# Replicating 1/std of one batch over the partitions: by two steps of small DMAs instead of six matmuls

## The chip, the cores and the metric

One core of a Trainium2 chip. The metric is device time of one execution in microseconds (us), lower is better. Differences are judged on runs of the fast state; a ratio is the mean time of one kernel's fast runs over that of the other's of the same rounds, so it is not quite the ratio of the medians that are quoted beside it.

Names used below: PE is TensorE, ACT ScalarE, DVE VectorE, POOL GpSimd, SP SyncE. "Landing" of a DMA is counted from its issue to the moment its last data is in place. "L476" is a line of the kernel that the line is from; the changed kernel is shorter, so the same statement has another number there.

## The reference, cut to what matters

```python
B, N, D = 2, 256, 1152
mod = (_silu(c) @ w_mod).reshape(B, 6, 1, D)
shift_a, scale_a, gate_a, ... = [mod[:, i] for i in range(6)]
h = _layernorm(x, axis=-1) * (1 + scale_a) + shift_a
qkv = h @ wqkv
q, k, v = ...
p = _softmax(jnp.einsum('bqd,bkd->bqk', q, k) * D ** (-0.5), axis=-1)
a = jnp.einsum('bqk,bkd->bqd', p, v) @ wo
return x + gate_a * a
```

All weights and x are bf16. h is kept transposed: features on the partitions, tokens along the free dimension. 1/std is one number per token. It comes out of ScalarE as a column, one token per partition, and is needed as a row that stands on all 128 partitions.

## The kernel before: the parts concerned

For batch 0 the kernel centres x, transposes it, and starts the key matmuls before 1/std is known (the keys of that batch are scaled later, in the scores). 1/std enters h by a multiply on DVE. The row for this multiply, `rep_sb`, is made by PE: POOL splits 1/std into three bf16 parts, and six matmuls with the identity replicate them and add them up in PSUM bank 7.

```python
def rep(b):                       # six matmuls
    for i in (2 * b, 2 * b + 1):
        for n in range(3):
            lhs = bass.AP(rpart_sb, n * TT + i, [[3 * TT, P], [0, P]])
            lo = NTOK + (i % 2) * P
            op(PE, lambda pe, ...: pe.matmul(ps[7][:, lo:lo + P], lhs, ident[:, :],
                                             start=(n == 0), stop=(n == 2)), ...)

def rep_out(b):                   # copy to SBUF
    op(AC, lambda a: a.activation(rep_sb[:, b * NTOK:(b + 1) * NTOK], ps[7][:, NTOK:2 * NTOK], ACT.Copy), ...)

def norm_x(cc, b):                # the multiply that needs it
    op(DVE, lambda e: e.tensor_tensor(dst, src, rep_sb[:, b * NTOK:(b + 1) * NTOK], ALU.mult), ...)
# ... [cut]
for g in range(2, len(SGROUPS)):  # key matmuls of columns 0..6, features k = 4..8
    for k in range(a, b_):
        for j in range(NA):
            qk_mm("ka", h0T_sb, "h0", DC + j, k, j)
            ...
        b = k - 6
        if b in CENTRED:          # after k = 6
            rep(b)
            rep_out(b)
            for cc in range(0, 6):
                norm_x(cc, b)
        if k == DC - 2:
            h_mm(0)               # shift of features 0, 1, into bank 7
h_ev(0)                           # DVE: copy of the shift, frees bank 7
# ... [cut]
for j in range(NA):
    qk_evac(j, DC + j, j)         # DVE and ACT in turn
shift_group(0)
for cc in range(6, 9):
    norm_x(cc, 0)
for n, bank in enumerate((7, 0)): # "kb": the last two key columns
    for k in range(DC):
        qk_mm("kb", h0T_sb, "h0", DC + NA + n, k, bank)
    qk_evac(n, DC + NA + n, bank)
# then the query matmuls, which read hT_sb
```

Each engine runs its own list in order, and a helper adds the semaphore waits. DVE's order: six multiplies, then the shift copy, then the key evacuations.

## Time and profile before

| | |
|---|---|
| time before, three runs | 98.52 us median (98.29 to 99.14) |
| execution that was profiled | 242.59 us, span 240.8 us, slow |
| PE busy in that profile | 237.4 us (99%) |
| six replicating matmuls in its chain | 1.00 us |

In a chain of waits a line is: start, length, what, xcount. In a timeline it is: start, length, engine, line, operation, output<-input, shapes, xcount, and in brackets how long the engine sat idle before and who ended that. The lines that matter are shown in the prediction. The odd thing is that the profiled execution took almost 2.5 times as long as the timed ones, with PE slow throughout. Its granted clock is printed as 1.0.

### The profile page before, as it was taken

To read this page: it belongs to the slowest core of one execution; us is meant where nothing else is said; L and a number is where in the kernel's file an instruction comes from. 1 tells how busy PE (TensorE), PEld (TensorE's weight loads), DVE (VectorE), ACT (ScalarE), POOL (GpSimd) and SP (SyncE) were. 2 spreads that over 40 slices of the span, in tenths; PEclk is the share of its full clock that TensorE was granted. 3 is DMA by queue.
4 is the path that set the end of the run, shared out by engine and by line. 5 is a ranking of instruction groups with operands and counts; after the bars stand their busy time and mean duration, and the time that the engine had idled before them with its cause. 6 is when DMAs were issued, how large, how long until landed. Compare 5 with 4: busy or idle time off the path is not lost.

```text
span 240.8 us, 1836 instructions
## 1 busy us (share of the span) xinstructions
PE 237.4 (99%) x738; PEld 99.8 (41%) x738; DVE 50.3 (21%) x136; ACT 29.7 (12%) x64; POOL 12.1 (5%) x35
## 2 busy tenths in 40 slices
PE   8999999999999999999999999999999999999996
PEld 1885543332233323222344644533345433333443
DVE  3550031055105000041000530000002212351212
ACT  4559000001000000020000220000003100000000
POOL 2221032000003000000000000000000000000000
DMA  6999999930005600000000010066400001010101
GB/s 214 334 330 323 377 362 380 390 139 0 0 0 179 262 3 0 0 0 0 1 0 0 14 33 0 0 29 39 33 0 0 0 16 33 16 33 16 35 16 33
DMA packets 20092, 21.91 MB, mean 91 GB/s; under 512 B 2034, under 2 KB 16114, under 8 KB 20084
## 3 DMA queue, kind: packets, MB, share of 16 engines
q1 hardware_dynamic: 19936, 21.50, 30.8%
q10 hardware_dynamic: 148, 0.30, 0.4%
q8 instruction: 6, 0.10, 0.2%
q14 instruction: 2, 0.02, 0.0%
HBM read 19.76 MB, written 1.18 MB: 87 GB/s over the span
## 4 chain that ended last, share of the span: by engine, by line
PE 99%; DVE 0%; issue 0%
PE psbank L561 40%; PE psbank L855 20%; PE psbank L739 20%; PE psbank L817 4%; PE psbank L752 4%; PE psbank L334 2%; PE psbank L395 2%; PE psbank L493 1%; PE psbank L796 1%; PE psbank L411 1%; PE psbank L516 1%; PE psbank L476 0%; PE psbank L576 0%; DVE xo_sb L860 0%; DVE warm_sb L322 0%
## 5 line engine op out<-in xcount | busy, mean ns | idle before, releaser
L561 PE MATMUL psbank<-pvT_sb,wq_sb 128*128 128x512 bf16 (+2 forms) x111 | 48.8, 666 | 0.0
L739 PE MATMUL psbank<-wq_sb,hT_sb 128*128 128x384 bf16 x108 | 48.8, 685 | 0.0
L561 PE MATMUL psbank<-hT_sb,wq_sb 128*128 128x512 bf16 x81 | 48.6, 833 | 0.0
L855 PE MATMUL psbank<-wm_sb,pvT_sb 128*128 128x384 bf16 x99 | 44.4, 687 | 0.0
L739 PEld LDWEIGHTS psbank<-wq_sb,hT_sb 128*128 128x128 bf16 x108 | 18.7, 174 | 29.4 <-issue 29.1
L561 PEld LDWEIGHTS psbank<-pvT_sb,wq_sb 128*128 128x128 bf16 x111 | 17.7, 171 | 25.8 <-issue 21.8
L855 PEld LDWEIGHTS psbank<-wm_sb,pvT_sb 128*128 128x128 bf16 x99 | 17.3, 175 | 26.7 <-issue 26.4
L561 PEld LDWEIGHTS psbank<-hT_sb,wq_sb 128*128 128x128 bf16 x81 | 13.8, 172 | 33.8 <-issue 33.4
L340 DVE CAST qkT_sb<-psbank 128x512 bf16<-128x512 f32 x10 | 6.9, 691 | 37.7 <-PE psbank L561 37.7
L340 DVE CAST v_sb<-psbank 128x384 bf16<-128x384 f32 x6 | 3.3, 557 | 47.7 <-PE psbank L739 47.7
L868 DVE TENSOR_TENSOR ga_sb<-psbank,gate_rep 128x384 bf16<-128x384 f32 x11 | 6.1, 557 | 32.3 <-PE psbank L855 32.3
L342 ACT ACTIVATE qkT_sb<-psbank 128x512 bf16<-128x512 f32 x8 | 4.8, 597 | 65.5 <-PE psbank L561 65.5
L752 PE MATMUL psbank<-qkT_sb 128*128 128x256 bf16 x36 | 10.9, 538 | 0.0
L817 PE MATMUL psbank<-pT_sb,v_sb 128*128 128x256 bf16 x36 | 10.9, 538 | 0.0
L752 PEld LDWEIGHTS psbank<-qkT_sb 128*128 128x128 bf16 x36 | 6.5, 181 | 4.5 <-issue 0.4
L817 PEld LDWEIGHTS psbank<-pT_sb,v_sb 128*128 128x128 bf16 x36 | 6.4, 177 | 4.6 <-issue 0.7
L342 ACT ACTIVATE v_sb<-psbank 128x384 bf16<-128x384 f32 x6 | 2.9, 490 | 36.1 <-PE psbank L739 36.1
L334 PE MATMUL psbank<-warm_sb 128*128 128x512 bf16 x9 | 5.6, 794 | 1.2 <-DVE warm_sb L322 1.2
L542 POOL TENSOR_SCALAR pvT_sb<-xnT_sb,s_sb 128x256 bf16<-128x256 bf16 (+1 forms) x9 | 4.9, 551 | 21.5 <-DVE s_sb L504 20.6
L493 PEld LDWEIGHTS psbank<-scT_sb,wm_sb 128*128 128x128 bf16 x99 | 4.6, 117 | 2.1 <-issue 1.8
L504 DVE TENSOR_SCALAR s_sb<-psbank 128x4 f32<-128x4 f32 (+1 forms) x4 | 0.6, 156 | 19.9 <-PE psbank L493 19.9
L487 DVE TENSOR_TENSOR hT_sb<-pvT_sb,rep_sb 128x256 bf16<-128x256 bf16 x9 | 3.2, 419 | 7.3 <-ACT rep_sb L481 7.3
(85 smaller groups left out, 103.4 us busy)
## 6 DMA issues: line engine op xcount, KB each, us to landing
wq_sb<-in_wqkv_dram SPq DMA_DIRECT2D x3, 864.0 KB, 10.8
wm_sb<-in_w_mod_dram SPq DMA_DIRECT2D x1, 2592.0 KB, 12.3
wm_sb<-in_wo_dram SPq DMA_DIRECT2D x1, 2592.0 KB, 9.3
wm_sb<-in_w_mod_dram SPq DMA_DIRECT2D x4, 576.0 KB, 7.6
wm_sb<-in_w_mod_dram SPq DMA_DIRECT2D x1, 2016.0 KB, 9.8
wq_sb<-in_wqkv_dram SPq DMA_DIRECT2D x2, 672.0 KB, 10.4
wq_sb<-in_wqkv_dram SPq DMA_DIRECT2D x2, 576.0 KB, 11.9
out_dram<-xo_sb SPq DMA_DIRECT2D x11, 96.0 KB, 1.6
```

Source lines behind the costliest of these rows:

```text
L334: op(PE, lambda pe: pe.matmul(ps[bank][:, 0:512], warm_sb[:, 0:P], warm_sb[:, 0:512], start=True, stop=True), r=[("warm",)], w=[("ps", bank)])
L340: op(DVE, lambda v: v.tensor_copy(dst, src), r=r, w=w)
L342: op(AC, lambda a: a.activation(dst, src, ACT.Copy), r=r, w=w)
L395: op(PE, lambda pe, cc=cc, bank=bank, lo=lo, src=src: pe.transpose(psb[bank][:, lo:lo + P], src[:, i, cc * P:(cc + 1) * P], ident[:, :]), ...
L493: op(PE, lambda pe, cc=cc, k=k: pe.matmul(ps[7][:, col + 2 * cc:col + 2 * cc + 2], src[:, k, (cc - base) * P:(cc - base + 1) * P], scT_sb[ ...
L542: op(POOL, lambda g: g.tensor_scalar(dst, src, sc, 0.0, op0=ALU.mult, op1=ALU.add), r=rk, w=wk)
L561: op(PE, lambda pe: pe.matmul(ps[bank][:, lo:hi], wq_sb[:, k, col * P:(col + 1) * P], src[:, k, lo:hi], start=(k == 0) if start is None el ...
L739: op(PE, lambda pe, k=k, q=q, bank=bank: pe.matmul(ps[bank][:, 0:384], hT_sb[:, k, i * P:(i + 1) * P], wq_sb[:, k, 2 * D + q * 384:2 * D + ...
L752: op(PE, lambda pe, cc=cc: pe.matmul(ps[bank][:, 0:NTOK], qkT_sb[:, cc, i * P:(i + 1) * P], qkT_sb[:, DC + cc, b * NTOK:(b + 1) * NTOK], s ...
L817: op(PE, lambda pe, h=h, cc=cc, sbk=sbk: pe.matmul(ps[bank][:, h * NTOK:(h + 1) * NTOK], v_sb[:, 2 * b + sbk, cc * P:(cc + 1) * P], pT_sb[ ...
L855: op(PE, lambda pe, i=i, k=k, rhs=rhs, n=n, bank=bank: pe.matmul(ps[bank][:, 0:n], pvT_sb[:, k, i * P:(i + 1) * P], rhs, start=(k == 0), s ...
L868: op(DVE, lambda v, b=b, c0=c0, c1=c1, n=n, bank=bank, s=s: v.tensor_tensor(ga_sb[:, s, 0:n], ps[bank][:, 0:n], gate_rep[:, b, c0:c1], ALU ...
```

## The change

The intent is to take the replication off PE, the busiest engine, and off POOL and ACT. ScalarE's DMA queue writes 1/std of each of the two tiles as a row into partition 0 (128 elements of 4 bytes each). A third DMA then reads this row 128 times and writes it to all partitions. It is issued as soon as 1/std is ready.

```diff
-    rpart_sb = sb("rpart_sb", [P, 3, TT], bf16)
-    rres_sb = sb("rres_sb", [P, 2, TT], f32)
+    row_sb = sb("row_sb", [P, T], f32)
 ...
-    def parts(b):            # five POOL instructions [cut]
     def rep(b):
         for i in (2 * b, 2 * b + 1):
-            for n in range(3):
-                lhs = bass.AP(rpart_sb, n * TT + i, [[3 * TT, P], [0, P]])
-                lo = NTOK + (i % 2) * P
-                op(PE, ... pe.matmul(ps[7][:, lo:lo + P], lhs, ident[:, :], ...
-    def rep_out(b):          # copy from PSUM [cut]
+            row = bass.AP(row_sb, i * P, [[T, 1], [1, P], [1, 1]])
+            op(AC, lambda e, row=row, i=i: e.dma_start(row, rstd_sb[:, i:i + 1]),
+               r=[("rstd", i)], w=[("row", i)], dma=True)
+        src = bass.AP(row_sb, b * NTOK, [[T, 1], [0, P], [1, NTOK]])
+        op(AC, lambda e: e.dma_start(rep_sb[:, b * NTOK:(b + 1) * NTOK], src),
+           r=[("row", 2 * b), ("row", 2 * b + 1)], w=[("rep", b)], dma=True)
 ...
     for b in CENTRED:
-        parts(b)
+        rep(b)
 ...
             if b in CENTRED:
-                rep(b)
-                rep_out(b)
                 for cc in range(0, 6):
                     norm_x(cc, b)
```

More of the change, by code (lines that the diff above doesn't have):

```diff
@@ L452, in rstd_c @@
            r=[("lnv", i0), ("lnv", i0 + 1)], w=[("rstd", i0), ("rstd", i0 + 1)])
-    def parts(b):
-        i0, i1 = 2 * b, 2 * b + 2
-        def part(n, src, rk):
-            op(POOL, lambda g: g.tensor_scalar(rpart_sb[:, n, i0:i1], src, 1.0, 0.0, op0=ALU.mult, op1=ALU.add),
-               r=rk, w=[("rpart", n, b)])
-        def rest(n, src, rk):
-            op(POOL, lambda g: g.tensor_tensor(rres_sb[:, n, i0:i1], src, rpart_sb[:, n, i0:i1], ALU.subtract),
-               r=rk + [("rpart", n, b)], w=[("rres", n, b)])
-        rs = [("rstd", i0), ("rstd", i0 + 1)]
-        part(0, rstd_sb[:, i0:i1], rs)
-        rest(0, rstd_sb[:, i0:i1], rs)
-        part(1, rres_sb[:, 0, i0:i1], [("rres", 0, b)])
-        rest(1, rres_sb[:, 0, i0:i1], [("rres", 0, b)])
-        part(2, rres_sb[:, 1, i0:i1], [("rres", 1, b)])
     def rep(b):
         for i in (2 * b, 2 * b + 1):
-            for n in range(3):
-                lhs = bass.AP(rpart_sb, n * TT + i, [[3 * TT, P], [0, P]])
-                lo = NTOK + (i % 2) * P
-                op(PE, lambda pe, lhs=lhs, lo=lo, n=n: pe.matmul(
-                    ps[7][:, lo:lo + P], lhs, ident[:, :], start=(n == 0), stop=(n == 2)),
-                   r=[("rpart", n, b), ("ident",)], w=[("ps", 7)])
-    def rep_out(b):
-        op(AC, lambda a: a.activation(rep_sb[:, b * NTOK:(b + 1) * NTOK], ps[7][:, NTOK:2 * NTOK], ACT.Copy),
-           r=[("ps", 7)], w=[("rep", b)])
+            row = bass.AP(row_sb, i * P, [[T, 1], [1, P], [1, 1]])
[4 more added lines that the diff above has]
+           r=[("row", 2 * b), ("row", 2 * b + 1)], w=[("rep", b)], dma=True)
     def norm_x(cc, b):
```

## The prediction

In the prediction, terms of the sum are cut with it: a count of PE's time at an assumed full speed, which put PE's work at 86 of the 98.5 us, the start of the last two key columns ("kb") at 28.0 us and the six matmuls at 0.33 us; and a fall of PE's clock in the gap, of an assumed size. The sum came to 10.9 - 4.8 = 6.1 us of wait plus 1.7 us for the clock: +7.8 us, 106.3 us, of which 105.6 was put down.

> **What bounds the kernel now.** I read the page's engine table first, then the chain of work that ended last in order of time, then the timeline around the removed work, and last the transfers, one window at a time. All are of the profiled execution.
>
> ```profile
> span 240.8 us, 1836 instructions
> PE 237.4 (99%) x738; PEld 99.8 (41%) x738; DVE 50.3 (21%) x136; ACT 29.7 (12%) x64; POOL 12.1 (5%) x35
> ...
> 39.67 6.96 PE psbank L561 x12
> 46.64 1.00 PE psbank L476 x6
> 47.64 4.07 PE psbank L561 x7
> 51.71 0.51 PE psbank L493 x18
> 52.22 19.13 PE psbank L561 x32
> ...
> 73.68 44.04 PE psbank L561 x74
> ```
>
> The chain (start, length, what) is PE from end to end, and the six replicating matmuls (L476) are 1.00 us of it. But this execution took 242.59 us and the timed ones 98.52 us. In the last line 74 matmuls of 512 columns take 595 ns each: 0.86 columns per ns, although the granted clock is recorded as 1.0. So the profiled run had a slow PE, and its slack is not the slack of the timed runs. The main work of this prediction is to carry it over.
>
> **PE in the timed runs (estimate).** Streaming columns: key and query 162 x 512, V 108 x 384, scores and P·V 72 x 256, output 99 x 384 + 9 x 256 + 9 x 128, transposes, means and replication 60 x 128: 192,000 in all[...]. So PE is nearly gap-free here too, and a new wait on PE costs its full length.
>
> [...]the gate replication, the same form of access pattern, runs alone at
>
> ```profile
> DMA packets 102, 0.05 MB, mean 27 GB/s; under 512 B 10, under 2 KB 102, under 8 KB 102
> ...
> gate_rep<-gaterow_sb SPq DMA_DIRECT2D x8, 72.0 KB, 7.2
> ...
> DMA to landing us min/median/max: 4.8/7.2/9.7
> ```
>
> (first line: window 158 to 160 us, no other traffic), while weight loads reach 356 GB/s.[...]
>
> **The change part by part.**
>
> ```profile
> 23.15 0.29 ACT L449 ACTIVATE lnv_sb<-sq_sb,eps_sb 128x2 f32<-128x2 f32 x1
> 23.48 0.20 ACT L451 ACTIVATE rstd_sb<-lnv_sb 128x2 f32<-128x2 f32 x1
> ...
> 47.67 0.38 ACT L481 ACTIVATE rep_sb<-psbank 128x256 f32<-128x256 f32 x1 [23.99 <-PE psbank L476]
> 48.09 2.10 DVE L487 TENSOR_TENSOR hT_sb<-pvT_sb,rep_sb 128x256 bf16<-128x256 bf16 x6 [7.28 <-ACT rep_sb L481]
> 52.26 0.16 DVE L526 COPY sh_sb<-psbank 128x4 f32<-128x4 f32 x1 [2.06 <-PE psbank L493]
> 52.82 0.69 DVE L340 CAST qkT_sb<-psbank 128x512 bf16<-128x512 f32 x1 [0.40 <-PE psbank L561]
> ```
>
> Removed: five POOL instructions (about 1.1 us, off the path), six matmuls (1.00 us in the slow profile[...]), one ACT copy of 0.38 us. Added: two DMAs that each write 128 single floats into one partition, and, after ACT has waited for both, one DMA that reads this one partition 128 times: 128 x 1 KB = 128 KB. The change's short name counts them as two; the diff has three, in two dependent steps. Moved: the start of the replication, from the PE queue after the k=6 key matmuls to right after 1/std on ACT.
>
> Who waits: six DVE multiplies need the replica. DVE works in order, and behind them stand the shift copy (L526), which frees bank 7, and the first key evacuation, which frees bank 0. The next PE work, the last two key columns ("kb"), begins in bank 7. So the path is: 1/std, row DMAs, replica, six multiplies (2.10 us), copy 0.16, kb. A late replica stops PE even though PE never reads it.
>
> The time there is (timed runs, estimates).[...] In the profile 1/std is ready at 23.68 us; ACT's chain before it idled about 5 us for PE's transposes and means, of which I take off 3, as DVE and the loads hold the rest: 20.7 us. The window is 28.0 - 20.7 = 7.3 us; less 2.10, 0.16 and 0.2 of semaphores, the replica may take 4.8 us from 1/std without loss.
>
> The time it takes. Issue of the first row DMA 0.5 us (ACT's c load took 0.53, its x load 0.36). The second row lands about 2.5 us after its issue: the SBUF transposes in the trace land in 2.3, small stores in 1.4, and this one has loads beside it. The replica: the fastest gate DMA landed in 4.8 us with 72 KB, and 56 KB more at 29 GB/s are 1.9 us: 6.7 us. Beside the weights, which keep the engines full until about 50 us, I add 1 us. Sum with 0.2 for waits: 0.5 + 2.5 + 6.7 + 1.0 + 0.2 = 10.9 us.
>
> So kb starts 10.9 - 4.8 = 6.1 us late. The 0.33 us saved on PE lies in this wait and yields nothing.[...] Sum +7.8 us, 106.3 us. I take 105.6, since each latency could be smaller more easily than 1/std could be later.
>
> **The rivals.** (1) Hidden anyway: the replica lands inside the window, PE saves 0.33 us, 98.2 us. For it: in the profile 24 us lie between 1/std and its use, and the code issues the DMAs as early as it can. Against: that gap is made of slow matmuls; in the timed runs it shrinks to the window above[...]. (2) The stall without the clock loss, or a shorter chain (row 1.5, replica 5.5): kb 3 to 6 us late, 101.5 to 104.5 us. (3) The ScalarE queue fares worse than I assume beside the weights: SyncE's issues are backed up for several us each (two in 7.30 us), and if ACT's three issues wait likewise the chain grows by 3 to 5 us: 109 to 111 us. Against: at the start ACT's issues overlapped SyncE's and still took 0.53 and 0.36. (4) ACT itself becomes late, as it waits for the row DMAs in order: it has nothing to do for 24 us (profile) and some 7 us (timed), so no cost.
>
> **Range and chances.** The window is uncertain by about 1 us, the transfers by 3 either way, the clock loss by 1.7. Eight in ten: 101.8 to 110.0 us. Faster by over 2% is excluded by the size of the saving, but for a wrong model of the clock: 0.02. Within 2% needs rival 1 or a chain under 6.5 us: 0.10. Slower: 0.88.
>
> **What would show it.** If the next profile is as slow as this one, the replica should land near 35 us, long before its use; the multiplies start at about 41 us instead of 48, and the span falls by the 1.0 us of L476, to about 239.8, while the timed runs still get slower: the profile alone would then mislead. If it is at full clock, DVE should wait for the replica's DMA for over 4 us, and PE should idle about 6 us before the first kb matmul, with the replica landing 6 to 8 us after issue and the rows 2 to 3. I am wrong if the timed runs stay within 1 us of before, if the replica lands in under 4.5 us, or if PE's gap stands elsewhere than before kb.

## The result, and the profile after

The changed kernel takes 108.91 us (median of 6 runs, 108.13 to 109.64) against 98.77 us (median of 6, 98.29 to 99.94) of the kernel before: ratio 1.103, 95% interval 1.096 to 1.111. It is correct, and slower.

The page of the changed kernel (span 106.3 us), engine table and granted clock over the span in 40 slices (9 is 90% or more of full clock):

```profile
PE 92.5 (87%) x732; PEld 55.0 (52%) x732; DVE 48.2 (45%) x136; ACT 28.2 (26%) x63; POOL 11.4 (11%) x30
...
PEclk9999999999995579999999999999999999999999
```

The reader should see 13% of PE's span idle and a dip of the clock at slices 13 to 15, which is 32 to 40 us. The chain of waits of the changed kernel at that place:

```profile
20.08 0.21 ACT rstd_sb L450
...
20.32 0.54 ACTq L456
...
20.90 5.81 DMA row_sb<-rstd_sb
...
26.73 6.66 DMA rep_sb<-row_sb
...
33.42 2.10 DVE hT_sb L465 x6
35.52 0.08 DVE sh_sb L504
...
35.65 6.99 PE psbank L539 x25
```

The lines left out are steps of 0.02 to 0.04 us. In the slow profile of the kernel before this chain was PE from end to end. (In its full-speed profile the chain also passes through the copy of the replica and the multiplies, but PE works on beside them without a gap.) Now it leaves PE for 15 us: 1/std, the second row DMA (5.81 us), the replication (6.66 us), six multiplies, the shift copy, and only then PE goes on with the last two key columns. Seen from PE, in the timeline and in the table of stretches (busy us and instructions of each engine, granted clock, DMA share, GB/s), changed kernel:

```profile
26.00 1.67 PE L539 MATMUL psbank<-pvT_sb,wq_sb 128*128 128x512 bf16 x7
35.65 5.48 PE L539 MATMUL psbank<-pvT_sb,wq_sb 128*128 128x512 bf16 x18 [7.98 <-DVE sh_sb L504]
...
27.67:35.65 7.98, 0.00 (x1) 0.01 (x1) 2.23 (x8) 1.22 (x3) 0.00 (x0) 0.75 1.04 351
35.65:41.13 5.48, 5.48 (x19) 2.22 (x20) 4.53 (x11) 0.00 (x0) 0.48 (x1) 0.73 1.10 355
```

PE does nothing for 7.98 us, and the clock mean over the gap and over the 18 matmuls after it is 0.75 and 0.73. From the first of the 18 matmuls to the next one that follows them it takes 5.3 us (35.65 to 40.97), where the kernel before needs 3.9 (27.05 to 30.96, below).

For comparison, the kernel before at full speed (run again unchanged, see the first experiment; span 96.3 us):

```profile
19.50 0.20 ACT L451 ACTIVATE rstd_sb<-lnv_sb 128x2 f32<-128x2 f32 x1
...
23.80 0.38 ACT L481 ACTIVATE rep_sb<-psbank 128x256 f32<-128x256 f32 x1 [4.09 <-PE psbank L476]
24.21 2.10 DVE L487 TENSOR_TENSOR hT_sb<-pvT_sb,rep_sb 128x256 bf16<-128x256 bf16 x6 [2.26 <-ACT rep_sb L481]
...
25.56 5.56 PE L561 MATMUL psbank<-pvT_sb,wq_sb 128*128 128x512 bf16 x25
```

From 1/std (19.70) to the replica (24.18) it takes 4.5 us, and 25 key matmuls, seven of k=8 and eighteen of the last two columns, run in one go: the last two columns start at 25.56 + 7 x 0.213 = 27.05 us.

So the 10.0 us between the spans (106.3 and 96.3) divide like this. The last two key columns start at 35.65 instead of 27.05: 8.6 us. Of these, 0.6 us are a later 1/std (20.28 instead of 19.70), and 8.0 lie between 1/std and the columns (15.37 us instead of 7.35). From there to the first query matmul it takes 5.3 us instead of 3.9: 1.4 us of lower clock (5 tenths in slices 13 and 14 of the row PEclk, so half). From the first query matmul to the last DVE instruction both need 63.4 us. The 0.6 us is there before the new DMAs move any data, so it is not theirs. In the traces of the experiments on the changed kernel 1/std is ready at other times again, at 19.47 us in x8 and at 21.65 us in x9, so this is scatter from one execution to the next.

The profiled execution is also the fastest of the six (108.13 us), and it lost least to the clock: its mean granted clock is 0.968, that of the other runs 0.952. By an estimate from these means, with all that is missing put down to half clock, that is (1 - 0.968) x 106.3 x 2 = 6.8 us at half clock in the profiled run and about 10.3 us in the others. So the 1.4 us is a low value: in x2 and x9, which have gaps of 7.32 and 7.16 us at the same place, it takes 5.9 and 5.8 us from the first of the 18 matmuls to the next one that follows them, a loss of 2.0 and 1.9 us.

### The profile page after: what moved, and what is told of

It reads as the page before. It is cut to its first block, busy times and chain, and to the rows that moved or that the text cites. A ratio compares the mean times of both kernels' runs of the same rounds, so it can differ in the third digit from the quotient of the medians.

```text
span 106.3 us, 1821 instructions
## 1 busy us (share of the span) xinstructions
PE 92.5 (87%) x732; PEld 55.0 (52%) x732; DVE 48.2 (45%) x136; ACT 28.2 (26%) x63; POOL 11.4 (11%) x30
## 4 chain that ended last, share of the span: by engine, by line
PE 65%; DMA 16%; ACT 8%; DVE 5%; issue 2%; ACTq 1%; POOL 1%
PE psbank L539 22%; PE psbank L715 17%; PE psbank L831 17%; DMA rep_sb<-row_sb 6%; DMA row_sb<-rstd_sb 5%; DMA x_sb<-in_x_dram 4%; PE psbank L793 4%; PE psbank L728 4%; DVE hT_sb L465 2%; ACT junk_sb L441 2%; ACT junk_sb L432 2%; DVE xnT_sb L428 1%; PE psbank L772 1%; ACT xnT_sb L341 1%; PE psbank L494 1%
## 5 line engine op out<-in xcount | busy, mean ns | idle before, releaser
L539 PE MATMUL psbank<-pvT_sb,wq_sb 128*128 128x512 bf16 (+2 forms) x111 | 20.0, 336 | 8.0 <-DVE sh_sb L504 8.0
L539 PEld LDWEIGHTS psbank<-pvT_sb,wq_sb 128*128 128x128 bf16 x111 | 9.8, 100 | 16.5 <-DVE sh_sb L504 8.5
L715 PE MATMUL psbank<-wq_sb,hT_sb 128*128 128x384 bf16 x108 | 18.1, 326 | 0.0
L539 PE MATMUL psbank<-hT_sb,wq_sb 128*128 128x512 bf16 x81 | 17.8, 379 | 0.0
L831 PE MATMUL psbank<-wm_sb,pvT_sb 128*128 128x384 bf16 x99 | 16.3, 326 | 0.0
L715 PEld LDWEIGHTS psbank<-wq_sb,hT_sb 128*128 128x128 bf16 x108 | 10.5, 98 | 7.1 <-DVE v_sb L339 0.2
L831 PEld LDWEIGHTS psbank<-wm_sb,pvT_sb 128*128 128x128 bf16 x99 | 9.7, 98 | 6.3
L539 PEld LDWEIGHTS psbank<-hT_sb,wq_sb 128*128 128x128 bf16 x81 | 7.9, 98 | 9.5 <-issue 0.2
L465 DVE TENSOR_TENSOR hT_sb<-pvT_sb,rep_sb 128x256 bf16<-128x256 bf16 x9 | 3.2, 423 | 10.9 <-DMA rep_sb<-row_sb 10.9
L793 PE MATMUL psbank<-pT_sb,v_sb 128*128 128x256 bf16 x36 | 4.1, 272 | 0.0
L728 PE MATMUL psbank<-qkT_sb 128*128 128x256 bf16 x36 | 4.1, 272 | 0.0
```

The source lines that it names most:

```text
L539: op(PE, lambda pe: pe.matmul(ps[bank][:, lo:hi], wq_sb[:, k, col * P:(col + 1) * P], src[:, k, lo:hi], start=(k == 0) if start is None el ...
L715: op(PE, lambda pe, k=k, q=q, bank=bank: pe.matmul(ps[bank][:, 0:384], hT_sb[:, k, i * P:(i + 1) * P], wq_sb[:, k, 2 * D + q * 384:2 * D + ...
L728: op(PE, lambda pe, cc=cc: pe.matmul(ps[bank][:, 0:NTOK], qkT_sb[:, cc, i * P:(i + 1) * P], qkT_sb[:, DC + cc, b * NTOK:(b + 1) * NTOK], s ...
L793: op(PE, lambda pe, h=h, cc=cc, sbk=sbk: pe.matmul(ps[bank][:, h * NTOK:(h + 1) * NTOK], v_sb[:, 2 * b + sbk, cc * P:(cc + 1) * P], pT_sb[ ...
L831: op(PE, lambda pe, i=i, k=k, rhs=rhs, n=n, bank=bank: pe.matmul(ps[bank][:, 0:n], pvT_sb[:, k, i * P:(i + 1) * P], rhs, start=(k == 0), s ...
```

## The experiments

Twelve kernels were run, in three groups on three chips; each group has its own runs of the kernel before, with medians of 98.28, 98.34 and 98.71 us. An experiment's profile is one execution, and 1/std comes at a slightly different time in each. My theory: the replica comes too late, since two dependent DMAs beside the weight loads take 13 us, PE stands still behind DVE's order, and the clock falls in the gap. Rivals: something else stops PE (weights, traffic); the small DMAs are slow in themselves; the replication is bound by reading one partition.

### b_again: the kernel before once more, for a profile at full speed

No edit.

> The kernel before, unchanged, to get its profile with a PE at full speed. My account of the timed runs says: 1/std of batch 0 ready at 20 to 21 us, the replica by matmul and copy ready at about 25 us, the last two key columns begin at 28.0 us, and no gap of PE over 1 us after 12 us. If the 8 us stall of the changed kernel is not caused by the late replica, a gap of PE should stand before those columns here too.

Measured (one look): 98.2 us. 1/std is ready at 19.70 us, the replica at 24.18, the last key columns start at 27.05 instead of 28.0, and PE has no gap of a microsecond before them. The window from 1/std to those columns is 7.35 us; the prediction had worked out 7.3. In the changed kernel there is a gap of 7.98 us at this place, and here none.

### x1_probe: the same DMAs in a quiet stretch

```diff
+    probe_row(prow1_sb, P, 0)                 # one row DMA, after the first V tile and the scores
     for i in range(TT):
         softmax(i, sbanks[i]); p_T(i)
+        if i == 0: ...  dma_start(prep_sb, row read 128 times)
+        if i == TT - 1: probe_row(prow2_sb, NTOK, 0); probe_row(prow2_sb, NTOK, 1)
```

> The changed kernel with three more copies of its DMAs in the quiet stretch after the weight loads, into unused tiles: one row DMA alone, one replication alone, two row DMAs together. If the weight backlog on the shared DMA engines makes them slow (my theory), the row lands in about 2 us instead of 5.8 and the replication in 3 to 4.5 us instead of 6.7. If the 128 writes of 4 bytes into one partition are slow in themselves, the row takes 5 us here too.[...]

Measured (one look, 108.26 us). DMA issues of this run: destination<-source, issuing queue, count, KB each, median us from issue to landing:

```profile
rep_sb<-row_sb ACTq DMA_DIRECT2D x1, 128.0 KB, 6.7
prep_sb<-row_sb ACTq DMA_DIRECT2D x1, 128.0 KB, 6.7
...
prow_sb<-rstd_sb ACTq DMA_DIRECT2D x3, 0.5 KB, 2.3
row_sb<-rstd_sb ACTq DMA_DIRECT2D x2, 0.5 KB, 6.0
```

The lines with a "p" are the probes, after the weight loads. A row DMA lands in 2.3 us when the queue is quiet and in 6.0 us at its real place. The 4-byte writes are thus not what costs; the place beside the weight loads is (x8 tests this in place). In the changed kernel no packet of the ScalarE queue moved between 20 and 23 us, so none until 2.1 us after the second issue. The replication is the other case: 6.7 us in both places. My expectation of 3 to 4.5 us for it was wrong. In the quiet place a limit on the reads of one partition or a fixed cost would explain it (x11 looks into that); that the time beside the weights is the same does not show the same cause there (see x9).

### x2_hold: later loads held until the replica has landed

```diff
-    load_w("qa", 0, 1, 0, NA * P); load_h(1); ... load_w("v", ...)      # at the start
+    rep(0); op(SP, None, extra=[replica DMA]); load_w("qa", 0, 1, ...); load_h(1); ...
```

> The changed kernel with all loads behind the last key weights held back until the replica has landed, so that the queue runs empty while the small DMAs go. Backlog theory: rows land in 3 to 4 us, the replica in 4 to 5, the stall of PE before the last key columns falls from 8.0 to 2 to 4 us, no loss of clock after it, and the time falls to about 102 to 104 us, unless the held loads come late themselves. Rival (slow in themselves): chain of 13 us as before, no gain, and the held loads cost several us more: 112 us or above.

Measured: 108.22 us (4 runs, 107.79 to 108.33), ratio 1.100 (1.097 to 1.103). No gain: a miss, and an instructive one.

```profile
rep_sb<-row_sb ACTq DMA_DIRECT2D x1, 128.0 KB, 6.3
row_sb<-rstd_sb ACTq DMA_DIRECT2D x2, 0.5 KB, 5.5
```

The rows are no faster, since when they were issued 1.2 MB of shift and key weights were still in the queue ahead of the hold. The replication ran in an emptied queue (28 GB/s in all between 28 and 30 us) and still took 6.3 us. Both readings of this run agree with the probe, but the run did not do what I built it for; x8 comes closer.

### x7_onestep: one DMA of the two steps

Wrong result on purpose (relative error 0.06).

```diff
+    memset(row_sb[0:1, 0:NTOK], 20.0)            # POOL, at the start
-        for i in (...): dma_start(row, rstd_sb[:, i:i + 1])
         dma_start(rep_sb, row read 128 times)    # still waits for 1/std
```

> Wrong result on purpose: the row DMAs are taken out, the replication reads a row filled with the constant 20 and still waits for 1/std. It leaves one DMA of the two dependent steps. If each step costs 6 us under load, the replica lands at about 27 us, the multiplies end at 29.2 and PE stalls about 1.7 us: 100 to 101 us. If the replication alone is what is too slow[...], the stall stays above 4 us: 104 us or more.

Measured: 99.70 us (4 runs, 99.31 to 99.98), ratio 1.014 (1.011 to 1.017).

```profile
rep_sb<-row_sb ACTq DMA_DIRECT2D x1, 128.0 KB, 6.6
...
28.53 4.06 PE L536 MATMUL psbank<-pvT_sb,wq_sb 128*128 128x512 bf16 x18 [0.91 <-DVE sh_sb L501]
```

With one step the replica lands 6.6 us after issue, PE waits 0.91 us, the clock does not fall (18 matmuls in 4.06 us), and the ratio falls from 1.103 to 1.014: 8.8 of the 10.2 us are gone. So it is the sum of two steps that breaks the window, not the replication alone. And one step of 6.6 us is still too slow for a gain.

### x3_warm: PE kept busy through the gap

```diff
+    for _ in range(40):
+        op(PE, ... pe.matmul(ps[7][:, 128:512], warm_sb[:, 0:P], warm_sb[:, 0:384], start=True, stop=True))
     h_ev(0)
```

> The changed kernel with 40 matmuls of 384 columns on zeros, into unused columns of bank 7, put between the end of the key matmuls and the copy of the shift, so PE is busy for 6.5 us of its 8 us gap. Clock theory: the last two key columns run at 216 ns per matmul instead of about 427 at first, 3.9 us instead of 5.5, and the time falls by 1.6 us, from 108.3 to 106.7. Rival (the half clock costs nothing, as DVE sets the pace there): no change within 0.3 us. If the dummy matmuls themselves delay the copy, the time rises instead.

Measured: 106.58 us (4 runs, 106.41 to 106.85), ratio 1.083 (1.081 to 1.086). Its timeline:

```profile
26.95 6.66 PE L659 MATMUL psbank<-warm_sb 128*128 128x384 bf16 x40
...
35.73 3.83 PE L539 MATMUL psbank<-pvT_sb,wq_sb 128*128 128x512 bf16 x17 [2.11 <-DVE sh_sb L504]
```

The dummy matmuls do no work that counts, and the last key columns start at about the same time (35.5; the first record is missing). Yet they end earlier: after a pause of 2.11 us they run at the pace of the kernel before (3.9 us for the 18), and the first query matmul comes at 39.40 us instead of 40.97. That is 1.6 us, of which 0.15 come from an earlier start; the ratio falls from 1.103 to 1.083, which is 2.0 us, as the timed runs of the changed kernel lose more to the clock than its profile. A loss near the 1.7 us that the prediction put down for the clock is shown.

### x4_order: the multiplies behind the evacuations on DVE

```diff
         if b in CENTRED:
-            for cc in range(0, 6): norm_x(cc, b)
 ...
     for j in range(NA): qk_evac(j, DC + j, j)
+    for cc in range(0, 6): norm_x(cc, 0)
     shift_group(0)
```

> The changed kernel with the six multiplies moved on DVE behind the shift copy and the key evacuations, so that only what really reads the replica waits for it. If PE is stopped through DVE's order (bank 7 freed late), the last two key columns start at about 27.7 us at full clock, the gap of PE moves behind them and shrinks to about 5 us, half clock then hits the first query matmuls: about 105.3 us. If PE is stopped by something else (weights, queue), nothing changes: 108.3 us.

Measured: 105.03 us (4 runs, 104.45 to 105.19), ratio 1.066 (1.063 to 1.069).

```profile
25.34 5.55 PE L539 MATMUL psbank<-pvT_sb,wq_sb 128*128 128x512 bf16 x25
...
36.06 1.03 PE L539 MATMUL psbank<-hT_sb,wq_sb 128*128 128x512 bf16 x2 [5.17 <-DVE hT_sb L530]
...
39.16 1.17 PE L494 MATMUL psbank<-wm_sb,scT_sb 128*32 128x224 bf16 x36
```

The replica comes no earlier, but the last key columns now run straight on (25 matmuls from 25.34 us), and the gap, 5.17 us, stands before the first query matmuls, which truly read it. The seven query matmuls from 36.06 to 39.16 us take 443 ns each on average against 216 in the kernel before, half clock again. So in the changed kernel PE was held by DVE's order, through bank 7, and not by data it needed.

### x5_nomm: all that there was to gain

Wrong result on purpose (relative error 0.06).

```diff
-        parts(b)
+        op(POOL, ... memset(rep_sb[:, 0:NTOK], 20.0))
-                rep(b)
-                rep_out(b)
```

> Wrong result on purpose: the kernel before with the parts, the six matmuls and the copy taken out and the replica set to the constant 20 early. It shows all that the change could ever have gained. PE spent 0.35 us of the chain on the six matmuls in the full-speed profile: 97.9 to 98.0 us, ratio 0.996. If the copy or the parts had been on the path too, more: ratio below 0.99.

Measured: 97.86 us (6 runs, 97.72 to 98.35), ratio 0.9955 (0.993 to 0.998). A replica that costs nothing and is there at once gains 0.45%, the 0.35 us of six matmuls and little more.

### x6_both: the DMAs as traffic alone

```diff
         parts(b)
+        rep_unused(b)   # two row DMAs into row_sb, one replication of a preset row into rep2_sb
```

> The kernel before with its replication by matmul, plus the three DMAs of the change into unused tiles (the replication from a preset row, so that ACT doesn't wait for the row DMAs). It shows what the DMAs cost as traffic alone. Waiting theory: nothing, 98.3 to 98.6 us. Contention theory: weights delayed enough to stop PE, 100 us or more. The row DMAs should land in about 6 us here too.

Measured: 101.94 us median of 6 runs (100.72 to 102.93), ratio 1.030 (1.025 to 1.035). Two of the six are counted as slow and left out of the ratio. My expectation of no cost was wrong; the rows landed in 5.7 us, as expected. DMA traffic from 22 to 30 us, first the kernel before (full speed), then this run:

```profile
q1 hardware_dynamic: 2273, 2.84, 107.5%
```

```profile
q1 hardware_dynamic: 1472, 1.37, 54.0%
q10 hardware_dynamic: 432, 0.13, 44.0%
...
36.03 1.05 PE L520 MATMUL psbank<-wm_sb,scT_sb 128*32 128x224 bf16 x36 [2.31 <-DMA wm_sb<-in_w_mod_dram]
```

q1 is SP's weight queue (packets, MB, share of the 16 engines' time), q10 ScalarE's. In these 8 us the weights moved 1.37 MB instead of 2.84, while q10 moved 0.13 MB and took 44% of the engines' time. The weights fall behind by 1.47 MB, some 4 us at their rate, and PE waits 2.31 us for the shift weights (last line, timeline). So the DMAs have a second price. In the changed kernel it does not show: no wait for weights follows the gap, and from the first query matmul on it needs the same 63.4 us as the kernel before. I take it that the weights catch up while PE stands still; that was not tested.

### x12_traffic2: the same traffic, read from two partitions

```diff
-   one replication of 128 KB that reads partition 0
+   two of 64 KB that read partitions 0 and 64
```

> The kernel before with the unused DMAs of the traffic run, but with the replication cut in two that read partitions 0 and 64. In the traffic run the weight queue moved only 0.16 MB between 24 and 28 us, against 1.5 MB in the kernel before, and PE waited 2.3 us for the shift weights. [...]100 to 100.5 us instead of 101.9, and a wait of about 1 us. If the number of descriptors does it, the time stays at 101.5 to 102.5.

(The 100 to 100.5 us stand for the case that reading one partition holds the engines.)

Measured: 100.07 us median of 6 runs (98.65 to 100.98); three of the six count as slow, and the kernel before scattered more on this chip too (98.25 to 100.37). Fast runs: ratio 1.002 (0.995 to 1.008). The traffic from 22 to 30 us:

```profile
q1 hardware_dynamic: 1984, 2.35, 93.5%
q10 hardware_dynamic: 576, 0.13, 13.2%
```

The same 0.13 MB now take 13.2% of the engines' time instead of 44%, and the weights lose 0.49 MB instead of 1.47. PE had no wait for the shift weights. That reading one partition is what holds the engines agrees with this, and the number of packets doesn't: there are more of them here (576 against 432). How a read of one partition would hold them these runs don't show. The times alone, on a restless chip, would carry less.

### x11_probe2: replications in a quiet stretch, by partition

```diff
+    probe(half_sb, 64 KB from partition 0)
+    probe(two_sb, 64 KB from partition 0); probe(two_sb, 64 KB from partition 64)
+    probe(same_sb, 64 KB from partition 0); probe(same_sb, 64 KB from partition 1)
```

> The changed kernel with replications from preset rows in the quiet stretches, into unused tiles. [...]with 2.2 us fixed and 29 GB/s for one partition: 64 KB alone 4.4 us; two of 64 KB together from partitions 0 and 64 4.4 to 5 us each; two of 64 KB together from partitions 0 and 1 up to 6.7 us for the later one. If the DMA count or the fixed cost rules, all are alike.

Measured (one look, 109.22 us), DMA issues of this run:

```profile
two_sb<-prow_sb ACTq DMA_DIRECT2D x2, 64.0 KB, 4.7
same_sb<-prow_sb ACTq DMA_DIRECT2D x2, 64.0 KB, 6.9
half_sb<-prow_sb ACTq DMA_DIRECT2D x1, 64.0 KB, 4.3
```

4.3 us alone, 4.3 and 5.2 for two from partitions 0 and 64, 6.5 and 7.3 for two from partitions 0 and 1. With 128 KB in 6.7 us that is 64 KB in 2.4 us more, by an estimate from these two times 27 GB/s and about 1.9 us fixed. So in a quiet queue the numbers fit a limit on the reads of one partition, which 0 and 64 don't share, and 128 KB from one partition moved at 26 to 30 GB/s there (x1, 68 to 71 us). The pair from partitions 0 and 1 is the weaker half of the evidence: it ran beside gate replication and output stores (47 to 141 GB/s in all between 85.9 and 96.7 us), the other probes nearly alone (8 to 60 GB/s between 64.4 and 72.5 us, their own bytes included). That 0 and 1 share a limit is thus not shown.

### x9_split: two partitions at the real place

```diff
-            row = bass.AP(row_sb, i * P, ...)
+            row = bass.AP(row_sb, (i % 2) * 64 * T + i * P, ...)     # tile 1 into partition 64
-        one replication of both rows
+        for i in (...): one replication of 64 KB, waits for its own row
```

> The changed kernel with the second row written to partition 64 and the replication cut in two DMAs of 64 KB, each reading its own partition. [...]4.4 to 5 us from issue to landing instead of 6.7, and the time falls by about 2 us, to 106.3. If it is the wait in the queue or a fixed cost, it stays at 6.5 or more and the time at 108.3.

(The 4.4 to 5 us and the 106.3 us stand for the case that reading one partition holds the replication.)

Measured: 108.68 us (4 runs, 107.48 to 109.11), ratio 1.098 (1.090 to 1.106); one run counts as slow and the verdict as unclear.

```profile
rep_sb<-row_sb ACTq DMA_DIRECT2D x2, 64.0 KB, 6.3
row_sb<-rstd_sb ACTq DMA_DIRECT2D x2, 0.5 KB, 5.0
```

Another miss. The time alone says little here: in the profiled execution 1/std came only at 21.65 us, 1.4 us later than in the changed kernel, and from there to the replica it took 12.0 us instead of 13.1, most of the gain in the rows (5.0 us). But two halves of 64 KB from two partitions land in 6.3 us beside the weights, hardly sooner than 128 KB from one partition (6.7). In the quiet queue this took 4.3 to 5.2. So beside the weights something else than the read of one partition sets most of the time; I take it for the wait in the queue. In the changed kernel, too, the replication's packets are recorded only from 30 us on, over 3 us after issue, and then most of them within 2 us (0.11 MB between 30 and 32 us), faster than the 27 GB/s of the quiet stretch. How reading and waiting overlap there is not settled by these runs.

### x8_holdrows: loads held until the rows have landed

```diff
-    load_h(0); load_w("kb", ...); load_w("qa", ...); ...                # at the start
+    rep(0); op(SP, None, extra=[both row DMAs]); load_h(0); load_w("kb", ...); ...
```

> The changed kernel with all loads behind the last key weights held back only until the two row DMAs have landed. The first hold failed to empty the queue for the rows, as 1.2 MB more were still in it. Backlog theory: the rows land in 3 to 4 us instead of 5.8 to 6, the replica still takes 6.7, the last key columns start 2 to 3 us earlier: 105.5 to 106.5 us, as long as their own weights, now issued at about 24 us, are there in time. If the rows stay at 5.5 us or more, backlog is not what slows them in place.

Measured: 105.92 us (4 runs, 104.72 to 106.74), ratio 1.070 (1.062 to 1.077); one run counts as slow, the verdict as unclear.

```profile
row_sb<-rstd_sb ACTq DMA_DIRECT2D x2, 0.5 KB, 3.4
...
30.17 0.64 PE L461 MATMUL psbank<-scT_sb,wm_sb 128*128 128x2 bf16 x18 [5.46 <-DMA wm_sb<-in_w_mod_dram]
```

With little left in the queue (207 GB/s between 18.2 and 20.8 us, 8 GB/s from there to 23.4) the rows land in 3.4 us instead of 5.8 to 6.0 at the same place in the program: backlog is shown as the cause in place of most of the delay. The replica still takes 6.5 us. The chain from 1/std to the replica shrinks from 13.1 us to 10.4 (19.47 to 29.84). But PE now waits 5.46 us for the first shift weights, which were held: the gain has turned into a new wait.

No version of the change with a right result beats the kernel before; the best was x4 with 105.03 us. And x5 bounds what any could gain at 0.45%.

## Why the prediction was right, by its steps

- **The reading of the profile.** The prediction took the profiled execution for a slow PE and rebuilt the timed one by count of columns. The full-speed profile bears it out: the window between 1/std and the last key columns is 7.35 us (predicted 7.3), the multiplies and the shift copy take 2.10 and 0.16 us, and PE has no large gap. Absolute times were about 1 us late (28.0 against 27.05, 20.7 against 19.7), which cancels; that the two errors are of one size is luck, as the 3 us taken off ACT's chain was a guess (4.0 it was). The full speed that the prediction assumed for PE is now measured: 26 matmuls of 512 columns (one record is missing) start from 25.56 us up to the next at 31.17, one per 216 ns. One reading was wrong: the clock of 1.0 in the slow profile was no record.
- **The saving.** 0.33 us predicted, 0.35 in the chain, and x5 measures 0.45%. It is lost inside the wait, as said.
- **The mechanism.** PE waits behind DVE, for bank 7, although it needs nothing of the replica: in x4, with another order on DVE, the 25 key matmuls run without a gap (25.34 us to 30.89).
- **The row DMAs: the term that was mis-sized.** 2.5 us predicted, 5.8 measured. The 2.5 was right for a quiet queue (2.3 in the probe). The allowance for the loads, put at 1 us for the whole chain, was too small: for the rows alone it is 3.5 us (x1; x8 takes back 2.4 of it). The prediction had assumed that the ScalarE queue need only share with the weights, which no trace had shown; its first packet moved 2.1 us after the second issue or later, and the rows then took until 26.7 us. At the same place they landed in 5.0 us in x9 and in 6.3 us in x11 (medians). Rival 3 foresaw the direction, and its lower end, 109 us, is nearer to the measured 108.91 than the 105.6 put down. Its reason, slow issues on ACT, did not come: they took 0.54 to 0.62 us.
- **The replication.** 6.7 us plus 1 for the loads predicted, 6.7 measured in all. The rate of 29 GB/s behind it is near what the quiet stretch shows (26 to 30 GB/s in x1, 27 by the estimate from x11); beside the weights the number was met by another mix of waiting and moving, which is in part luck. The 27 GB/s that the prediction read off for the gate DMAs are one window of several: from 162 to 170 us the same DMAs moved 39 to 53 GB/s. They read partitions 0, 32, 64, 96 and the next of each, so more than one may have been read at a time then; this was not taken apart.
- **The sum.** Chain 10.9 us predicted, 13.1 measured (20.28 to 33.39). PE late by 6.1 us predicted, by 8.6 measured with 0.6 of it not from the DMAs. Half clock 1.7 us predicted, 1.4 measured in the profile after a gap of 7.98 us, 2.0 and 1.9 after 7.32 and 7.16 us (x2, x9). So it does not follow the length of the gap there; after 2.11 and 0.91 us (x3, x7) the 18 matmuls took the 3.9 us of the kernel before. In all +7.8 by the sum and +7.1 as put down (105.6), +10.1 measured by the medians of 98.77 and 108.91. The measured time lies in the range, near its upper end; taking off 0.7 us, from 106.3 to 105.6, went the wrong way.
- **What it did not see.** The traffic of the replication delays the weights (x6). By this, rival 1, "hidden anyway, 98.2 us", would probably not have come out as put: in x6, where nothing waits for the DMAs, they still cost 3.0%.

The prediction also named a trap: had the next profile been a slow one again, it might have shown a gain. That could not be tried, as the next profile was fast.

## What to carry to other kernels

Before moving work from a busy engine to DMAs, count the dependent DMA steps and give each the landing time of small transfers beside the load that runs then, not in a quiet queue (here 6 us against 2.3), and set their sum against the window read from a profile at the speed of the timed runs. A wait shows up where the in-order engine behind it holds a buffer, not only where the data is read; ordering that engine's list by who truly needs the data took the ratio from 1.103 to 1.066 here. The broadcast that read one partition was slow itself (128 KB in 6.7 us) and also robbed the loads beside it (1.37 MB instead of 2.84 in 8 us). Reading partitions 0 and 64 instead gave the loads back most of that (2.35 MB, x12), but beside the loads it did not bring the replica much sooner (6.3 us, x9).
